# Eight 48-wide heads laid in natural order with zero padding, loads over two queues, and a new order of single operations, in a recurrence with a bilinear layer behind it

## The chip, the cores and the metric

The kernel runs on one core of one Trainium2 chip. The metric is the device time of one execution in microseconds (us). Most executions of one kernel agree within 0.3 to 1%; some fall into a slower state with a lower granted clock on the matrix engine, and each run is marked fast or slow. Only fast runs are compared. Names: PE is TensorE (matmuls; PEld is its weight load), DVE is VectorE, ACT is ScalarE, POOL is GpSimd, SP is SyncE, and a "q" after a name means that engine's instruction queue, where it also issues DMA transfers.

## The reference

For each of 4 batches and 8 heads, a 48 x 48 state decays row by row with `alpha`, takes an outer product, and is read by the query, over 768 steps. The features of the eight heads, 384 in all, then pass a bilinear layer.

```python
B, H, S, D = 4, 8, 768, 48
for t in range(S):
    state = alpha[:, :, t, :, None] * state + einsum('bhd,bhe->bhde', k[:, :, t], v[:, :, t])
    y[:, :, t] = einsum('bhd,bhde->bhe', q[:, :, t], state)
x = y.transpose(0, 2, 1, 3).reshape(B * S, H * D)        # 3072 x 384
out = ((x @ w_a) * (x @ w_b)) @ w_out                    # 384 -> 1536 -> 384
```

## The kernel before

Both kernels cut the work into six chunks: chunk c handles two batches ("halves" 0 and 1) and 256 of the 768 steps. A chunk loads `a`, `k`, `q`, `v`, takes logarithms and prefix sums of the decays, multiplies `q` and `k` by them, and turns the products so that the feature dimension lies on the partitions. It then makes scores, masks them, adds the part carried in by the state, and gives features `xT`. Chunk c is a set of single steps; the bilinear part of earlier chunks fills TensorE between them.

The products of a chunk lie in `QKp`. There are two ways to turn them into `kqT`: eight TensorE transposes per half and per four heads, with a copy out of PSUM (`stC`), or one DMA transposition per half (`stT`), which costs TensorE nothing:

```python
def stC(ch, u, h, eng):
    t = bank("f", 4, BF16, [C, 2, 2, 2, C])
    for j, src in ((1, Kp[i]), (0, Qp[i])):
        for p in range(2):
            for r in range(2):
                nc.tensor.transpose(t[:, j, r, p], src[...], ident)
    ...                                      # copy to kqT on VectorE or ScalarE
def stT(ch, u, eng):                         # eng is SyncE
    eng.dma_start_transpose(out=alloc_t(ch, u).rearrange(...), in_=QKp[ch.c % 2][:, u].rearrange(...))
```

The decay of a whole half chunk reaches the state's layout either by 64 one-column matmuls or by a way over DRAM, on SyncE's queue too: two transfers `row <- beta`, then two `bl <- row`.

```python
def decay(ch):
    row = dram.tile([2, 2 * P2, 2, D], F32, name="row")
    for g in range(2):
        nc.sync.dma_start(out=row[g:g + 1]..., in_=ch.beta[(g + 1) * HC - 1:(g + 1) * HC, :, 1]...)
    for r in range(2):
        nc.sync.dma_start(out=bls[ch.c % 2][r * DP:r * DP + D]..., in_=row[:, :, r, :]...)
```

Heads sit in slots of 64 with 16 unused columns, so the last two heads' features must be moved into the gaps of the first six: the "gap" matmuls `stG`. The order of steps is a list per chunk of the bilinear part, of which these are some steps (cuts are marked by dots; the numbers of an entry are its place and its chunk; `T` is the DMA transposition, `C` the TensorE one, `dec D` the decay by DMA, `ld` a load, the last letter the engine):

```python
1: [... (14, 2, "C 0 0 V"), ..., (15, 2, "C 1 0 V"), ...          # chunk 2 turns on TensorE
    (18, 4, "new"), ..., (19, 4, "ld q * P"), (19, 4, "ld k * P"), ..., (20, 4, "ld v * P"), ...
    (25, 3, "mq 0 V"), (25, 3, "T 0 Y"), (26, 3, "mq 1 V"), (27, 3, "dec D"), (27, 3, "T 1 Y"), (27, 4, "ld a * P")],
```

Of the kernel before, what the change touches and what calls it, by code (L numbers as in the profile page):

```python
# [14 lines left out]
START = [  # L15
    (0, "new"), (0, "ln"), (0, "ld a 0 Y"), (0, "ld a 1 Y"), (0, "ld k 0 Y"), (0, "L 0 V"), (0, "ld q 0 Y"), (0, "warm 18"), (0, "ld v 0 Y"),
    (0, "ld k 1 Y"), (0, "ld q 1 Y"), (1, "new"), (0, "ld v 1 Y"), (0, "L 1 P"), (0, "A 0"), (0, "gate_w q 1"), (0, "W 0 512"), (0, "W 512 1024"),
    (1, "ld a * P"), (0, "W 1024 1536"), (0, "Wo 4 8"), (0, "Wo 0 4"), (0, "A 1"), (1, "ld v 0 P"), (0, "Wo 8 12"), (1, "ld k 0 P"),
    (1, "ld q 0 P"), (1, "ld q 1 P"), (0, "warm 24"), (1, "ld k 1 P"), (1, "ld v 1 P"), (0, "mk 0 V"), (0, "dec P"), (0, "v 0 S"), (0, "mq 0 V"),
    (0, "C 0 0 V"), (0, "warm 6"), (0, "C 0 1 S"), (0, "D 0 0 s2"), (0, "K 0 P y2"), (0, "warm 8"), (0, "warm 14"), (0, "v 1 S"), (0, "S 0"),  # L20
    (0, "mk 1 V"), (0, "D 0 1 s2"), (0, "mq 1 V"), (0, "warm 18"), (0, "Y 0 V"), (0, "C 1 0 V"), (0, "G 0 V"), (0, "D 1 0 s2"), (0, "C 1 1 S"),
    (0, "K 1 V y2"), (0, "ff 1 0"), (0, "ff 0 0"), (0, "S 1"), (0, "D 1 1 s2"), (0, "Y 1 S"), (0, "ff 3 0"), (0, "G 1 S"), (0, "ff 2 0"),
    (0, "ff 1 1"), (0, "ff 2 1"), (0, "ff 0 1"), (0, "ff 3 1"),
]



PLAN = {
    0: [(9, 1, "L * V"), (14, 1, "A 1"), (16, 1, "A 0"), (16, 1, "dec P"), (16, 2, "new"), (16, 2, "ld a * P"), (22, 2, "ld v * P"),
        (24, 1, "v 0 S"), (25, 1, "mk 0 V"), (25, 2, "ld k * P"), (25, 2, "ld q * P"), (25, 1, "mq 0 V"), (25, 1, "C 0 0 V"), (25, 1, "C 0 1 S"),  # L30
        (25, 1, "D 0 0 s2"), (25, 1, "K 0 P y2"), (26, 1, "mk 1 V"), (26, 1, "S 0"), (26, 1, "mq 1 V"), (26, 1, "D 0 1 s2"), (27, 1, "Y 0 S"),
        (27, 1, "v 1 S"), (27, 1, "C 1 0 V"), (27, 1, "C 1 1 V"), (27, 1, "G 0 S"), (27, 1, "D 1 0 s2"), (27, 1, "K 1 V y2"), (27, 1, "S 1"),
        (27, 1, "D 1 1 s2"), (27, 1, "ff 1 0"), (27, 1, "ff 3 0"), (27, 1, "Y 1 S"), (27, 1, "G 1 S"), (27, 1, "ff 0 0"), (27, 1, "ff 2 0")],
    1: [(0, 1, "ff 1 1"), (2, 3, "new"), (5, 1, "ff 3 1"), (5, 3, "ld k * P"), (5, 3, "ld a * P"), (6, 1, "ff 2 1"), (6, 2, "L * V"),
        (7, 3, "ld q * P"), (10, 1, "ff 0 1"), (10, 2, "A 0"), (10, 2, "A 1"), (11, 2, "mk 0 V"), (12, 2, "dec P"), (12, 3, "ld v * P"),
        (12, 2, "mq 0 V"), (13, 2, "mk 1 V"), (13, 2, "mq 1 V"), (14, 2, "C 0 0 V"), (14, 2, "v * S"), (15, 2, "C 0 1 S"), (15, 2, "C 1 0 V"),
        (15, 3, "L * P"), (16, 2, "D 0 0 s2"), (16, 2, "K * P"), (17, 2, "C 1 1 S"), (18, 2, "S 0"), (18, 4, "new"), (18, 2, "D 0 1 s2"),
        (19, 4, "ld q * P"), (19, 4, "ld k * P"), (20, 2, "D 1 0 s2"), (20, 2, "Y 0 S"), (20, 3, "A 0"), (20, 4, "ld v * P"), (21, 2, "G 0 V"),
        (21, 3, "mk 0 V"), (22, 3, "A 1"), (22, 2, "S 1"), (22, 2, "D 1 1 s2"), (23, 3, "mk 1 V"), (24, 2, "Y 1 S"), (25, 2, "G 1 S"),
        (25, 3, "mq 0 V"), (25, 3, "T 0 Y"), (26, 3, "mq 1 V"), (27, 3, "dec D"), (27, 3, "T 1 Y"), (27, 4, "ld a * P")],  # L40
    2: [(6, 3, "v * P"), (6, 3, "D 0 0 s2"), (8, 4, "L * P"), (9, 3, "K * V"), (10, 3, "S 0"), (10, 3, "D 0 1 s2"), (12, 5, "new"), (12, 3, "Y 0 S"),
        (13, 3, "D 1 0 s2"), (13, 3, "G 0 S"), (14, 4, "A 1"), (15, 3, "S 1"), (15, 3, "D 1 1 s2"), (16, 4, "A 0"), (16, 3, "Y 1 S"),
        (16, 4, "mk 0 V"), (19, 4, "mq 0 V"), (19, 4, "T 0 Y"), (20, 3, "G 1 S"), (22, 4, "mk 1 V"), (23, 4, "mq 1 V"), (24, 4, "v * S"),
        (24, 4, "dec D")],
    3: [(0, 4, "K * V"), (5, 5, "ld a * P"), (6, 5, "ld q * P"), (6, 4, "S 0"), (6, 4, "D 0 0 s2"), (7, 5, "ld v * P"), (7, 4, "D 0 1 s2"),
        (7, 5, "L * V"), (8, 4, "T 1 Y"), (9, 5, "ld k * P"), (11, 4, "D 1 0 s2"), (11, 4, "Y 0 S"), (12, 4, "G 0 S"), (12, 5, "A 0"),
        (13, 4, "S 1"), (13, 4, "D 1 1 s2"), (14, 5, "mk 0 V"), (14, 5, "A 1"), (15, 5, "mq 0 V"), (16, 4, "Y 1 V"), (16, 5, "dec D"),
        (19, 5, "mk 1 V"), (19, 4, "G 1 S"), (20, 5, "mq 1 V"), (20, 5, "T 1 Y"), (20, 5, "T 0 Y"), (26, 5, "v * V")],
    4: [(0, 5, "K * V"), (1, 5, "D 0 0 s2"), (6, 5, "D 1 0 s2"), (6, 5, "S 0"), (9, 5, "D 0 1 s2"), (12, 5, "Y 0 V"), (13, 5, "G 0 V"),
        (14, 5, "S 1"), (14, 5, "D 1 1 s2"), (17, 5, "Y 1 S"), (23, 5, "G 1 S")],  # L50
    5: [],
}


@with_exitstack
def kernel(
# [125 lines left out]
    def logs(ch, us, eng):  # L182
        if us.start == 0:
            alloc(ch)
# [301 lines left out]
```

## Time and profile before

| | before |
|---|---|
| time, median (range), first three runs | 224.5 us (222.9 to 227.1) |
| profiled span, granted clock | 222.4 us, 0.987 |
| TensorE busy | 199.5 us, 90% |
| bytes moved by DMA, packets | 30.70 MB, 37,874 |

The prediction below shows the lines that bound it, with their reading. First SyncE's queue (columns: start, time on the queue, engine, line of the kernel, operation, out<-in, how many):

```profile
99.08 3.12 SPq L264 DMA_TRANSPOSE kqT<-QKp  x1
...
104.81 1.31 SPq L221 DMA_DIRECT2D row<-beta  x2
107.34 0.93 SPq L224 DMA_DIRECT2D bl<-row  x2
```

The first DMA transposition of the whole kernel is issued at 99 us, when most of the ordinary loads are through, and holds the queue for 3.1 us.

### The profile page before, as it was taken

The page shows a single profiled execution, that of the slowest core. Times are in us where ns is not written, and L with a number is a line of the kernel's source. Part 1 is how long each engine was busy: PE and PEld are TensorE (multiplying, and loading weights), DVE is VectorE, ACT ScalarE, POOL GpSimd, SP SyncE. Part 2 cuts the span into 40 slices and gives each one's busy share as a digit, 9 for nine tenths or more (in the row PEclk, how much of TensorE's full clock was granted, in tenths as well). Part 3 has the DMA queues.
Part 4 walks back from the last instruction along what each step waited for, and adds up shares of the span by engine and source line. Part 5 has one row for each costly group of instructions (what it writes and reads, how often), then busy time and mean ns, then how long its engine had stood idle before and what let it go on. Part 6 is the DMA issues. An engine that isn't in the chain of part 4 may idle for free.

```text
span 222.4 us, 6004 instructions
## 1 busy us (share of the span) xinstructions
PE 199.5 (90%) x2558; PEld 118.5 (53%) x2584; DVE 132.0 (59%) x189; ACT 105.9 (48%) x195; POOL 55.7 (25%) x79
## 2 busy tenths in 40 slices
PE   3798799999799969899779999899999989999991
PEld 3487665566575545464345565464555445544460
DVE  5569657458736879942887914889508763045400
ACT  3470467742346955644517654577233334254420
POOL 8358949737200048400280000000000000000000
PEclk9999999999889999999999999999999999999997
DMA  7999999999999103999879945400881000320022
GB/s 168 261 175 154 200 181 168 271 266 323 325 282 259 38 3 82 265 271 180 65 173 264 197 114 113 93 0 4 126 172 37 3 3 0 83 58 3 0 71 71
DMA packets 37874, 30.70 MB, mean 138 GB/s; under 512 B 27084, under 2 KB 34008, under 8 KB 37848
## 3 DMA queue, kind: packets, MB, share of 16 engines
q0 software_dynamic: 8480, 19.27, 37.4%
q1 hardware_dynamic: 29368, 11.05, 25.6%
q8 instruction: 20, 0.33, 0.6%
q14 instruction: 6, 0.05, 0.1%
HBM read 25.97 MB, written 4.74 MB: 138 GB/s over the span
## 4 chain that ended last, share of the span: by engine, by line
PE 75%; DVE 12%; ACT 4%; issue 3%; DMA 2%; POOL 1%; SPq 1%; POOLq 0%; DVEq 0%; ACTq 0%
PE f L379 20%; PE f L360 19%; PE f L370 18%; PE f L207 4%; DVE m L282 4%; PE y L308 3%; PE s L281 3%; PE y L292 2%; PE f L254 1%; PE y L315 1%; DVE xT L297 1%; DVE kqT L260 1%; PE f L203 1%; DMA bl<-row 1%; DVE tmp L342 1%
## 5 line engine op out<-in xcount | busy, mean ns | idle before, releaser
L360 PE MATMUL f<-xT,wa_t 128*128 128x512 bf16 (+1 forms) x229 | 59.6, 361 | 1.2 <-ACT kqT L258 0.3
L370 PE MATMUL f<-xT,wb_t 128*128 128x512 bf16 (+1 forms) x225 | 59.0, 361 | 1.1 <-issue 0.5
L379 PE MATMUL f<-wo_t,prod 128*128 128x384 bf16 x288 | 48.6, 326 | 0.7 <-DVE prod L372 0.7
L379 PEld LDWEIGHTS <-prod 128*128 128x128 bf16 x288 | 27.8, 98 | 19.7 <-DVE prod L372 1.1
L360 PEld LDWEIGHTS <-wa_t 128*128 128x128 bf16 x240 | 22.5, 99 | 21.2 <-issue 1.0
L370 PEld LDWEIGHTS <-wb_t 128*128 128x128 bf16 x240 | 22.4, 99 | 21.2 <-issue 1.3
L282 DVE TENSOR_TENSOR m<-s,mask 128x1024 bf16<-128x1024 f32 x24 | 29.3, 1222 | 4.3 <-PE s L281 4.0
L381 ACT ACTIVATE ot<-f 128x384 f32<-128x384 f32 x24 | 11.8, 490 | 35.0 <-PE f L379 34.9
L187 POOL TENSOR_TENSOR l<-la 128x768 f32<-128x768 f32 (+1 forms) x3 | 4.6, 1532 | 41.1 <-ACT la L185 22.3
L299 ACT ACTIVATE xT<-y 128x256 bf16<-128x256 f32 (+1 forms) x18 | 10.7, 596 | 8.6 <-PE y L308 5.6
L207 PE MATMUL f<-l,ut_f 128*128 128x384 f32 x24 | 11.1, 562 | 3.6 <-DVE l L187 3.6
L215 DVE TENSOR_TENSOR QKp<-k_t,invb 128x768 bf16<-128x768 f32 x12 | 12.4, 1036 | 1.0 <-ACT invb L211 1.0
L281 PE MATMUL s<-kqT 64*64 64x128 bf16 x384 | 11.5, 222 | 1.4 <-DVE kqT L260 0.7
L215 DVE TENSOR_TENSOR QKp<-q_t,beta 128x768 bf16<-128x768 f32 x12 | 11.6, 977 | 0.5 <-DMA q_t<-in_q_dram 0.5
L342 DVE TENSOR_TENSOR tmp<-s,S 128x384 f32<-128x384 f32 x4 | 2.2, 558 | 15.5 <-PE s L329 15.5
L281 PEld LDWEIGHTS <-kqT 64*64 64x64 bf16 x384 | 7.7, 106 | 6.0 <-issue 3.9
L210 ACT ACTIVATE invb<-f 128x384 f32<-128x384 f32 x12 | 5.9, 492 | 10.0 <-DVE le L208 10.0
L185 ACT ACTIVATE la<-a_t 128x1536 f32<-128x1536 f32 (+1 forms) x7 | 9.1, 1295 | 3.1 <-DMA a_t<-in_alpha_dram 3.1
L208 DVE TENSOR_TENSOR le<-f,la 128x384 f32<-128x384 f32 x12 | 6.7, 556 | 4.9 <-PE f L207 4.7
L258 ACT ACTIVATE kqT<-f 128x1024 bf16<-128x1024 bf16 x5 | 5.1, 1022 | 9.0 <-PE f L254 8.9
L292 PE MATMUL y<-kqT,S 64*64 64x128 bf16 x96 | 7.0, 221 | 2.4 <-DVE tmp L342 1.5
L308 PE MATMUL y<-m,vx 64*48 64x128 bf16 x384 | 7.7, 220 | 1.6 <-DVE m L282 1.6
(233 smaller groups left out, 280.7 us busy)
## 6 DMA issues: line engine op xcount, KB each, us to landing
out_dram<-ot SPq DMA_DIRECT2D x48, 96.0 KB, 2.2
a_t<-in_alpha_dram POOLq DMA_DIRECT2D x5, 768.0 KB, 12.5
v_t<-in_v_dram POOLq DMA_DIRECT2D x4, 768.0 KB, 13.6
k_t<-in_k_dram POOLq DMA_DIRECT2D x4, 768.0 KB, 14.0
q_t<-in_q_dram POOLq DMA_DIRECT2D x4, 768.0 KB, 13.5
wo_t<-in_moe_w_out_dram POOLq DMA_DIRECT2D x3, 384.0 KB, 6.7
wa_t<-in_moe_w_a_dram POOLq DMA_DIRECT2D x6, 144.0 KB, 4.2
wb_t<-in_moe_w_b_dram POOLq DMA_DIRECT2D x6, 144.0 KB, 4.4
```

The lines of the kernel that those rows point to most:

```text
L185: nc.scalar.activation(out=ch.la[:, us].rearrange("p b h r d -> p (b h r d)"), in_=ch.a[:, us].rearrange("p b h r d -> p (b h r d)"), func ...
L207: nc.tensor.matmul(p, lhsT=ut_f32, rhs=ch.l2[:, u].rearrange("p h d -> p (h d)"), start=True, stop=True)
L215: eng.tensor_mul(dst[ch.c % 2][:, u, :, :, :D], src[:, u].rearrange("p h r d -> p r h d"), by[:, u])
L281: nc.tensor.matmul(s2[g * HC:(g + 1) * HC, r, p, rk, :], lhsT=keysT(ch, u, 2 * h + p, g, r, rk), rhs=queriesT(ch, u, 2 * h + p, g, rs), st ...
L282: nc.vector.tensor_mul(m.rearrange("p r a k s -> p (r a) (k s)"), s2.rearrange("p r a k s -> p (r a) (k s)"), maskn(4))
L292: nc.tensor.matmul(y[rs, g, p, :], lhsT=lhsT, rhs=queriesT(ch, u, p, g, rs), start=(p == 0), stop=False, skip_group_check=True)
L299: nc.scalar.activation(out=o_, in_=i_, func=AF.Copy)
L308: nc.tensor.matmul(ch.y[u][r * DP:r * DP + D, g, p, :], lhsT=ch.vx[g * HC:(g + 1) * HC, u, 2 * p + r, rk, :], rhs=ch.m[u, p // 2][g * HC:( ...
L360: nc.tensor.matmul(ap, lhsT=wa_t[:, kk, f * 128:(f + 1) * 128], rhs=ff_x(ch, us)[:, kk], start=(kk == 0), stop=(kk == KT - 1))
L370: nc.tensor.matmul(bp, lhsT=wb_t[:, kk, f * 128:(f + 1) * 128], rhs=ff_x(ch, us)[:, kk], start=(kk == 0), stop=(kk == KT - 1))
L379: nc.tensor.matmul(op, lhsT=ch.prod[:, f, m * C:(m + 1) * C], rhs=wo_t[:, f, :], start=(f == 0), stop=(f == NFF - 1))
L381: nc.scalar.activation(out=ot, in_=op, func=AF.Copy)
```

## The change

The intent is less work for TensorE and a denser start. Heads lie in natural order, 48 wide, in three tiles of 128; values and states are padded with zeros, so a head that straddles a multiple of 64 is made in two pieces and the gap matmuls go. Chunk 0 is loaded half by half over SyncE's and GpSimd's queues. Most products of `q` and `k` move from VectorE to GpSimd, chunk 2 turns by DMA as well, and the order of everything is one list of single operations over all chunks.

```diff
-    def stG(ch, u, eng):
-        for t in range(KT):
-            for g in range(2):
-                nc.tensor.matmul(ch.y[u][:, g, t, :], lhsT=gap[:, t]..., rhs=ch.xT[:, KT, 2 * g + u, :], ...)
+    PIECES = [(h, j) for h in range(H) for j in range(D * h // DP, (D * h + D - 1) // DP + 1)]
+    def inner(ch, u):
+        for n in reversed(range(len(PIECES) // 2)):
+            for rk in range(2):
+                for c in range(2):
+                    h, j = COLS[c][n]
+                    at = h * VS + DP * j - D * h
+                    for g in range(2):
+                        out_mm(ch, u, g, h, j, vx[gs, u, rk, at:at + DP], ch.m[u, h // 4][gs, h % 2, h // 2 % 2, rk, :])
...
-    (0, "ld a 0 Y"), (0, "ld a 1 Y"), (0, "ld k 0 Y"), (0, "L 0 V"), (0, "ld q 0 Y"), (0, "warm 18"), ...
+0: c1; warm 70 0; cz 0 V; cz 1 V; cs 0 V; cs 1 V
+0: ld a 0 Y; ld k 0 Y; ld q 0 Y; ld a 1 P; ld v 0 Y; ld k 1 P
...                                              (from here on cut to the lines of 60 to 115 us that matter here)
+2: dec
+2: mk 1 P
+4: ld k * P
+2: T 0
+4: ld q * P
+2: T 1
+3: E 0 b0; le 1; E 1 i1; mq 0 P; mk 0 V
+3: E 1 i0; mq 1 P; T 0
+3: dec
+3: mk 1 P
+4: ln *; ld v * P
+3: T 1
+5: ld a * P
+5: ld k * P
+3: D 0 0 4
+5: ld q * P
```

In this list the number ahead of the colon is the chunk, `mq`/`mk` the query and key product of a half, `T` its DMA transposition, `D` its scores, `dec` its decay by DMA, `P`, `V`, `S`, `Y` the engine.

## The prediction

> **What bounds the kernel now.** I read the page's busy line and the chain of waits first, then the chain in order of time, then busy time by stretches, then the timeline of the start.
>
> The page names TensorE, and the chain agrees:
>
> ```profile
> PE 199.5 (90%) x2558; PEld 118.5 (53%) x2584; DVE 132.0 (59%) x189; ACT 105.9 (48%) x195; POOL 55.7 (25%) x79
> ...
> PE 75%; DVE 12%; ACT 4%; issue 3%; DMA 2%; POOL 1%; SPq 1%; POOLq 0%; DVEq 0%; ACTq 0%
> ```
>
> Matmul ends are modelled, so for costs I take the steps in the chain in order of time (start, length, what), which are start to start:
>
> ```profile
> 12.26 0.83 PE s L236 x64
> ...
> 36.57 0.65 PE f L370 x3
> ...
> 37.86 0.65 PE f L207 x2
> ...
> 47.87 0.46 PE f L254 x8
> ...
> 116.27 0.44 PE y L315 x6
> ...
> 126.38 7.80 PE f L379 x48
> ...
> 145.06 0.45 PE y L308 x32
> ...
> 165.41 0.83 PE s L329 x55
> ...
> 170.99 0.45 PE y L292 x16
> ```
>
> So three 512-column matmuls cost 0.65 us; one prefix sum (L207, two halves) 0.65; eight transposes 0.46; six gap matmuls (L315) 0.44; 48 output matmuls 7.80; 32 value matmuls (L308) 0.45, 14 ns each; 16 carried-state matmuls (L292) 0.45, 28 ns each. Sum for the whole kernel: 144 groups of three give 93.6, 288 output matmuls 46.8, twelve prefix sums 7.8, twelve groups of transposes 5.5, 24 of scores at about 0.43 (estimate, from their 16 in 0.42 to 0.45) 10.3, L292 5.4, L308 5.4, L315 5.3, the state products about 5.0, decays on TensorE 3 x 0.83 = 2.5. **Total 187.6 us of TensorE demand** in a span of 222.4; 140.4 of it, the bilinear part, no change of layout can touch.
>
> Where are the other 35 us? In the start, in stalls, and in the tail. The stretches (columns: us, then busy time and instructions of PE, PEld, DVE, ACT, POOL, granted clock, DMA share, GB/s):
>
> ```profile
> 54.00:60.00 6.00, 4.38 (x139) 3.40 (x136) 4.06 (x7) 2.42 (x4) 3.26 (x3) 0.97 1.05 333
> 60.00:66.00 6.00, 5.51 (x69) 4.12 (x66) 2.39 (x4) 2.51 (x6) 0.00 (x0) 0.74 1.05 292
> 66.00:80.00 14.00, 12.95 (x156) 7.71 (x157) 11.34 (x19) 11.85 (x22) 0.00 (x0) 1.00 0.52 131
> 80.00:98.00 18.00, 15.63 (x286) 9.63 (x281) 14.71 (x18) 8.71 (x19) 9.49 (x8) 1.00 0.63 159
> 98.00:114.00 16.00, 13.68 (x169) 6.98 (x170) 8.72 (x11) 6.40 (x10) 4.15 (x4) 1.00 0.86 140
> 217.90:222.40 4.50, 0.00 (x0) 0.00 (x0) 0.00 (x0) 0.48 (x1) 0.00 (x0) 0.74 0.30 72
> ```
>
> The tail is 4.5 us. TensorE becomes dense only when the second half of the first chunk's features is ready, at 28.6 us (the chain's last "ACT xT L299" of the start is at 27.75, 0.82 long). By then it has done about 9.4 us of chunk 0's recurrence and eight half groups of the bilinear part at 0.325, 2.6 us: 12.0. From 28.6 to 217.9 are 189.3 us for the remaining 175.6, so **stalls and slow clock are about 13.7 us**. One clear stall is at 109.8 to 112.1, where carried-state matmuls wait for a state whose decay came by DMA: the chain has SPq 0.69, row 1.67, bl 2.30, DVE Sm 1.90 in a row there.
>
> **What the skill says.** (1) "TensorE: Matmul & The Clock Gate", Part 1: the array runs at half rate until it has been busy for about 3.4 us and falls back after such an idle window. The trace agrees: the first 18 warm-up matmuls take 2.10 us (117 ns each), the array then idles from 3.5 to 7.0, and the first two prefix sums take 2.90 us instead of 2 x 0.65. (2) "DMA: Bandwidth & Descriptors", Specifications: transfers under 512 B are below line rate. Inputs come in pieces of 384 B; they moved at 261 GB/s between 6 and 12 us, while 333 appear at 54 to 60. (3) "SBUF — State Buffer", "Who interferes with whom": a VectorE instruction with two SBUF inputs and a GpSimd instruction reading SBUF exclude each other. I use it for a rival; no view of before isolates it.
>
> **The change, part by part.**
>
> TensorE demand. The eight heads of 48 features are laid at their natural place in three tiles of 128, so a head that straddles a 64 boundary is computed in two pieces with zero padding: twelve pieces in place of eight heads. Counted from the instruction order of both kernels:
> - gap matmuls 72 to 0: minus 12 x 0.44 = -5.3
> - transposes on TensorE 96 to 64 (chunk 2 now by DMA too): -4 x 0.46 = -1.8
> - value matmuls 384 to 576: +192 x 0.014 = +2.7
> - carried-state matmuls 192 to 240. Before, each used the diagonal quarters only (input half equals output half), 28 ns; now input and output halves cross, four quarters in turn as in L308, so 14 ns (estimate): 3.4 for 5.4, -2.0
> - state products 384 to 320: -64 x 0.013 = -0.8; decay on TensorE three chunks to two: -0.8
>
> Sum **-8.0**, demand 179.6. The bilinear part only changes a few full groups into halves, at no cost (0.325 twice is 0.65).
>
> VectorE. 15 of 24 input multiplications go to GpSimd (15 x about 1.0 = -15), five PSUM copies of transposes go (-3.4), the split copies of y become single (-1.3), nine output copies come (+5), state multiplications come back from GpSimd (+3.5): about 121 for 132. ACT loses nine 0.38 copies of y, nine of 0.49 of the output and most casts of v: about 95. GpSimd gains 15 multiplications of perhaps 1.8 us (it took 1.80 for the addition of 768) to about 75. None comes near 180, so none of this counts by itself; only where they sit in a chain.
>
> The start. (a) l2 of chunk 0 still starts near 6.3 us: the mask copy (1.88) goes, but VectorE now clears both buffer sets (0.48 + 0.4 + 0.07 + 0.8 + 0.4, twice, 4.3 us, scaled from before's memsets). (b) 70 warm-ups hold TensorE until about 6.6, so the prefix sum takes 0.65, not 1.45, and the exponentials begin straight after it at 7.7 rather than 9.26. (c) Operations are single, so query and key of half 0 are ready near 11.5 (before: 12.3, and then TensorE was in decays until 13.0), masks of half 0 end near 16.6 (18.96). (d) Chunk 1's first prefix sum stands ahead of Y 0 in TensorE's order; it needs chunk 1's alpha, the fifth block on the SP queue. At about 265 GB/s for both queues together (both are the same engines) 3.1 MB of chunk 0 are in at 14 us, alpha of chunk 1 near 15, its logarithm and GpSimd's pair sum near 17.5. So Y 0 near 19, features of half 0 near 21 (21.9 now), of half 1 near 24.5 (28.6 now). (e) Weights now load over 128 partitions in one transfer, not 48 and 16, but share the engines with chunk 1: at 14 us weights begin, and 0.39 MB each take about 2.2 us, so the first two quarters are in near 22.8, just in time.
>
> I choose **24.5 us for dense work**. By then TensorE has done 8.2 of chunk 0, 2.1 of chunk 1 and seven half groups, 2.3: 12.6. Left: 179.6 - 12.6 = 167.0. Stalls: before 13.7; the new order interleaves two or three chunks' bilinear work between single steps, but TensorE is in order and each step's engine must be on time; I choose 11, in which 1.5 for waits on weights and the clock's dip. 24.5 + 167.0 + 11 + 4.5 = **207.0**.
>
> **The rivals.**
> - Loading becomes the wait. Chunk 1's inputs now compete with weights between 14 and 30 us; if 265 GB/s is all there is, 6.3 MB of two chunks plus 3.1 of early weights need until about 37 us. If the order needs them earlier, dense work starts near 30 and the time is 212 to 216. For it: DMA share is full in the first 72 us now. Against: weights in narrow transfers now reach only 173 to 187 GB/s.
> - GpSimd becomes the late partner: 15 multiplications on the slower engine, behind DMA issues of about 1.1 us each and excluded by VectorE. Each late key or query delays transposes by DMA (4.5 us). Then stalls stay at 13 or more: 210 to 214.
> - Everything is on time: stalls fall to 4, as between 160 and 217.9 now, where TensorE idles only 1.4 of 57.9 us. Then 200.
> - The granted clock falls as TensorE gets denser. The clock was 0.74 in 60 to 66 us, once; one or two more such dips cost about 1.5 us each.
>
> **Range and chances.** The TensorE saving is nearly certain and alone makes 216; the start adds 3 to 5, the order 0 to 10. Range 200 to 216. Slower needs both first rivals at full size: 0.01; within 2% 0.03; faster 0.96.
>
> **What would show it.** Right: no gap matmuls; carried-state groups at about 14 ns each; prefix sum of chunk 0 at 0.65; dense bilinear matmuls from about 24 us; TensorE idle under 9 us from there to the end. Wrong: TensorE waits on wa, wb or chunk 1's alpha before 35 us; GpSimd as releaser of TensorE or of the DMA transposes; a second clock dip; value matmuls above 14 ns, since they load weights 64 wide for pieces partly zero.

## More of the kernel before

Second the stretch from 26 to 40 us (columns as in the prediction: us, then busy time of PE, PEld, DVE, ACT, POOL with counts, granted clock, DMA share, GB/s):

```profile
26.00:40.00 14.00, 13.65 (x171) 8.81 (x173) 7.17 (x13) 9.84 (x20) 10.82 (x16) 1.00 1.07 197
```

TensorE is full there: 13.65 of 14 us.

## The result, and the profile after

| | before | after |
|---|---|---|
| time, median (range) of 4 runs | 224.89 us (222.94 to 227.13) | 231.68 us (230.98 to 258.82) |
| fast runs | all four | 231.72, 231.64, 230.98 (the fourth, 258.82, is slow: clock 0.892) |
| profiled span, clock | 222.4 us, 0.987 | 229.9 us, 0.963 |

The ratio is 1.032, 95% interval 1.023 to 1.041: the kernel is slower, where 207 us and faster had been predicted. Ratios in this document are the mean time of one kernel's fast runs over that of the other's from the same rounds, so not quite the ratio of the medians that I quote. Results are correct in every run unless I say otherwise.

The page of the changed kernel: busy time, forty slices of TensorE, clock and DMA in tenths, and the chain of waits by engine.

```profile
PE 196.6 (85%) x2641; PEld 118.4 (51%) x2664; DVE 129.4 (56%) x189; ACT 94.7 (41%) x175; POOL 67.5 (29%) x68
...
PE   8868885989999956930799999899999999999992
...
PEclk9999999999999995895599999999999999999999
...
DMA  7999999999993999999417610431340230001235
...
PE 67%; DMA 15%; DVE 5%; issue 5%; SPq 3%; POOL 2%; ACT 1%; DVEq 0%; ACTq 0%; POOLq 0%
```

Busy time of TensorE did fall, though part of it ran at a lower clock. But DMA's share of the chain rose from 2% to 15%. The slices say where: each is 5.75 us, and in slices 15 to 20, some 80 to 115 us, TensorE shows 5, 6, 9, 3, 0, 7 tenths and a clock of half speed twice, while DMA is full in slices 14 to 19. By stretches:

```profile
26.00:40.00 14.00, 9.71 (x179) 7.13 (x178) 8.26 (x12) 5.47 (x16) 10.37 (x9) 1.00 1.22 235
80.00:98.00 18.00, 13.45 (x203) 7.55 (x202) 10.87 (x13) 7.46 (x15) 12.88 (x10) 0.81 1.06 265
98.00:114.00 16.00, 5.27 (x151) 3.16 (x150) 4.79 (x7) 2.04 (x4) 0.63 (x1) 0.69 0.92 169
114.00:126.00 12.00, 11.95 (x167) 6.57 (x167) 6.52 (x8) 6.57 (x11) 5.41 (x3) 0.98 0.37 68
160.00:200.00 40.00, 39.74 (x407) 21.11 (x405) 19.73 (x28) 13.63 (x24) 0.00 (x0) 1.00 0.23 49
```

Against the lines of before (13.65; 15.63; 13.68 in the first three), TensorE lost 3.9 us early and 10.6 us of busy time from 80 to 114, more in work, since a good part of what is left ran at half clock. From 114 on it is as dense as anyone could ask. So the loss is not dearer work on TensorE (196.6 us busy for 199.5, part of it at half clock); the change starved it, for the most part in one place.

What starved it is on SyncE's queue:

```profile
74.97 1.59 SPq L692 DMA_TRANSPOSE kqT<-QKp  x1
...
78.66 10.24 SPq L692 DMA_TRANSPOSE kqT<-QKp  x2
89.00 1.27 SPq L646 DMA_DIRECT2D row<-beta  x2
95.32 0.97 SPq L649 DMA_DIRECT2D bl<-row  x2
96.40 11.94 SPq L692 DMA_TRANSPOSE kqT<-QKp  x1
...
118.43 1.51 SPq L692 DMA_TRANSPOSE kqT<-QKp  x1
```

and beside it GpSimd's queue, where it issues loads:

```profile
75.58 1.19 POOL L594 DMA_DIRECT2D k_t<-in_k_dram  x1 [2.83 <-DVE vx L706]
76.76 1.15 POOL L594 DMA_DIRECT2D q_t<-in_q_dram  x1
...
86.67 1.20 POOL L594 DMA_DIRECT2D v_t<-in_v_dram  x1
87.86 1.15 POOL L594 DMA_DIRECT2D a_t<-in_alpha_dram  x1
89.00 1.15 POOL L594 DMA_DIRECT2D k_t<-in_k_dram  x1
90.92 1.16 POOL L594 DMA_DIRECT2D q_t<-in_q_dram  x1
```

The same instruction holds the queue for 1.5 to 1.6 us at 75 and at 118, when few loads move beside it, and for 11.94 us at 96, with five loads of 0.79 MB issued beside it since 86 (four are shown, the fifth comes at 97.5; 3.9 MB; at the 265 GB/s of that stretch some 15 us, an estimate). The line at 78.66 is two turns, of 7.23 and 2.84 us. SyncE issues in order, so what comes after waits too: the decay of chunk 3 is issued at 89.0, as soon as those two are through, and the turn at 96.4, as soon as the decay is. The small transfer of the decay is slow as well: its second step can start only 6.3 us after its first, when `row` has landed, where before took 2.5 (104.8 to 107.3). TensorE's own lines, from its timeline, and the chain's piece of the same wait:

```profile
88.42 0.64 PE L749 MATMUL psum<-kqT 64*64 64x128 bf16 x16 [4.04 <-DMA kqT<-QKp]
...
110.37 0.64 PE L749 MATMUL psum<-kqT 64*64 64x128 bf16 x16 [10.51 <-DMA kqT<-QKp]
```

```profile
89.68 5.62 DMA row<-beta
96.40 13.93 DMA kqT<-QKp
```

Score matmuls stood idle for 4.0 and 10.5 us, until transposed data had landed. From issue to use the last took 13.93 us, not the 4.5 that I had carried over from before. After each such wait the clock is down. For the second, in windows of the same trace:

```profile
98.00:104.00 6.00, 1.86 (x127) 1.41 (x124) 1.02 (x2) 2.04 (x4) 0.63 (x1) 1.00 1.06 246
104.00:106.00 2.00, 0.00 (x0) 0.00 (x0) 0.00 (x0) 0.00 (x0) 0.00 (x0) 0.53 1.04 223
106.00:114.00 8.00, 3.41 (x24) 1.75 (x26) 3.77 (x5) 0.00 (x0) 0.00 (x0) 0.50 0.79 98
```

the array is idle from about 100 and granted half speed from about 104 until after 113. That is what the Trainium skill says in "TensorE: Matmul & The Clock Gate", Part 1 (half rate after an idle window of about 3.4 us), and this wait agrees. The first does not quite: TensorE stopped at 84.4, and the clock was down from about 87.1, some 2.7 us later (0.77 in 86 to 88, 0.50 in 88 to 92).

One warning on reading: the page's list of DMA issues gives a median of 4.4 us to landing for the eight transposes, as in before. The median, and only those whose landing is matched, hide the slow ones; the queue and the chain show them.

### The profile page after: what moved, and what is told of

It reads as the page before. It is cut to its first block, busy times and chain, and to the rows that moved or that the text cites.

```text
span 229.9 us, 6120 instructions
## 1 busy us (share of the span) xinstructions
PE 196.6 (85%) x2641; PEld 118.4 (51%) x2664; DVE 129.4 (56%) x189; ACT 94.7 (41%) x175; POOL 67.5 (29%) x68
## 4 chain that ended last, share of the span: by engine, by line
PE 67%; DMA 15%; DVE 5%; issue 5%; SPq 3%; POOL 2%; ACT 1%; DVEq 0%; ACTq 0%; POOLq 0%
PE psum L816 37%; PE psum L839 18%; DMA a_t<-in_alpha_dram 6%; DMA kqT<-QKp 6%; PE psum L765 5%; DMA row<-beta 2%; PE psum L623 2%; DVE QKp L641 2%; PE psum L749 2%; POOL QKp L641 2%; SPq L594 1%; PE psum L720 1%; DVE vx L706 1%; DVE prod L829 1%; SPq L692 1%
## 5 line engine op out<-in xcount | busy, mean ns | idle before, releaser
L816 PE MATMUL psum<-xT,wa_t 128*128 128x512 bf16 (+1 forms) x233 | 54.8, 355 | 3.1 <-issue 1.5
L816 PE MATMUL psum<-xT,wb_t 128*128 128x512 bf16 (+1 forms) x236 | 55.0, 355 | 2.7 <-ACT as__815 L822 1.8
L839 PE MATMUL psum<-wo_t,prod 128*128 128x384 bf16 x288 | 54.5, 335 | 0.0
L754 DVE TENSOR_TENSOR m<-psum,mask 128x1024 bf16<-128x1024 f32 x24 | 29.1, 1223 | 18.0 <-PE psum L749 16.8
L641 POOL TENSOR_TENSOR QKp<-q_t,beta 128x768 bf16<-128x768 f32 x8 | 15.6, 1959 | 29.8 <-ACT beta L637 23.9
L749 PE MATMUL psum<-kqT 64*64 64x128 bf16 x384 | 10.6, 226 | 15.7 <-DMA kqT<-QKp 14.6
L641 POOL TENSOR_TENSOR QKp<-k_t,invb 128x768 bf16<-128x768 f32 x7 | 12.7, 1812 | 17.9 <-PE psum L816 17.9
L749 PEld LDWEIGHTS <-kqT 64*64 64x64 bf16 x384 | 7.3, 110 | 18.6 <-DMA kqT<-QKp 15.2
L619 PE MATMUL psum<-wz 128*128 128x128 bf16 x148 | 11.3, 243 | 1.0 <-DVE wz L542 1.0
L765 PE MATMUL psum<-m,vx 64*64 64x128 bf16 x576 | 10.9, 225 | 0.8 <-DVE m L754 0.8
L619 PEld LDWEIGHTS <-wz 128*128 128x128 bf16 x148 | 10.3, 111 | 1.6 <-DVE wz L542 1.0
## 6 DMA issues: line engine op xcount, KB each, us to landing
q_t<-in_q_dram POOLq DMA_DIRECT2D x4, 768.0 KB, 13.9
v_t<-in_v_dram POOLq DMA_DIRECT2D x4, 768.0 KB, 13.3
```

Of the source, the lines that this page charges most:

```text
L619: nc.tensor.matmul(w[:, :C], lhsT=wz, rhs=wz, start=True, stop=True)
L641: eng.tensor_mul(QKp[ch.c % 2][:, u, j, :, :, :D], src[:, u].rearrange("p h r d -> p r h d"), by[:, u])
L749: nc.tensor.matmul(s2[g * HC:(g + 1) * HC, r, p, rk, :], lhsT=ch.kqT[u][rs, 1, rk, 2 * h + p, g * HC:(g + 1) * HC], rhs=queriesT(ch, u, 2 ...
L754: nc.vector.tensor_mul(m.rearrange("p r a k s -> p (r a) (k s)"), ch.s2[u, h].rearrange("p r a k s -> p (r a) (k s)"), maskn(4))
L765: nc.tensor.matmul(y[c * DP:(c + 1) * DP, g, j // 2 * C:(j // 2 + 1) * C], lhsT=lhsT, rhs=rhs, start=(g, c) not in begun, stop=False, skip ...
L816: nc.tensor.matmul(p, lhsT=(wa_t, wb_t)[w][:, kk, f * 128:(f + 1) * 128], rhs=ch.xT[:, kk, us, :], start=(kk == 0), stop=(kk == KT - 1))
```

## The experiments

My theory, C: a transposition by DMA that meets ordinary loads is slow, it holds SyncE's queue, and TensorE waits. Rivals: G, GpSimd's slower products make the turns late; Q, the decay by DMA stands ahead of the turn on the same queue; and, for the first 40 us, L, the loads of chunk 1 hold up the features. Every edit is to the changed kernel unless I say otherwise. All ran for three rounds, one for five; each list of intervals is a 95% interval of the ratio to the kernel before. In the edits lines of the order are shown as above.

### 1. Loads later

```diff
-5: ld k * P        (some steps after 5: ld a * P)
-5: ld q * P        (some steps later)
-5: ld v * P        (later again)
+5: ld k * P; ld q * P; ld v * P     (after 4: mk 1 P, some 20 us later)
```

> Theory C (contention): in the changed kernel the DMA transposes of chunks 2 and 3 and the decay of chunk 3 share the DMA engines with bulk loads of chunks 4 and 5 (265 GB/s from 84 to 104 us), and take 10 to 14 us instead of 4.4. Here k, q and v of chunk 5 (2.4 MB, about 9 us of the engines at 265 GB/s) are issued later, behind GpSimd's last key product of chunk 4. C expects: the transpose issued near 96 lands within 6 us, TensorE's 10.5 us idle before the scores of chunk 3 shrinks below 4, the half clock after it goes, and the time falls by 8 to 12 us, to 220 to 224. Rival G (GpSimd's products are late): no part of them moves, so the time stays within 2 us of 231.7. Rival Q (the order on the SP queue: the decay's round trip stands ahead of the transpose): the order is the same, so the time stays within 3 us.

Measured: 225.27 us (224.23 to 227.31), ratio to before 1.003 [0.994, 1.013]. That transposition on the queue:

```profile
96.71 2.86 SPq L690 DMA_TRANSPOSE kqT<-QKp  x1
```

2.86 us in place of 11.94, at nearly the same moment, with the same instructions ahead of it. Some 6 us came back by moving three loads alone. C holds for this turn; the whole gain, 6.4 us, is less than the 8 to 12 expected, and waits for turned data of 7.3 us in three pieces, the longest 4.3, are left: chunk 4's loads still lie on the second turn of chunk 2 and the first of chunk 3.

### 2. Turns on TensorE

```diff
-2: T 1      -3: T 0      -3: T 1
+c: C u 0 t; C u 1 t+1; Ce u 0 S; Ce u 1 V     (c the chunk, u the half; each just ahead of that half's D, on the same banks)
```

> Three of the four transposes of chunks 2 and 3 go to TensorE (8 transposes of 0.46 us per half group, six half groups, 2.8 us) and their PSUM copies to ScalarE and VectorE in the same place, loads and everything else as in the changed kernel. C and Q both expect: no wait for a DMA transpose between 80 and 112 us; each of the three places now waits about 1.2 us for a copy; gain 10 to 13 us, to 219 to 222, with the decay of chunk 3 by DMA as the wait that remains. G expects the waits to stay, now on GpSimd's products, and a gain under 4 us.

Measured: 222.36 us (220.52 to 223.44), ratio 0.987 [0.979, 0.995], 9.3 us below the changed kernel and so just short of the 10 to 13 expected. TensorE does 14.38 us in 98 to 114, not 5.27:

```profile
98.00:114.00 16.00, 14.38 (x130) 7.59 (x133) 9.48 (x12) 7.87 (x13) 4.80 (x3) 0.89 0.68 144
```

So paying for three halves with TensorE's own time (six groups of eight, 0.46 us each, 2.8 us) is cheaper than waiting for the DMA engines.

### 3. The products back on VectorE

```diff
-3: mq 0 P   -3: mq 1 P   -3: mk 1 P
+3: mq 0 V   +3: mq 1 V   +3: mk 1 V
```

> The three products of chunk 3 that GpSimd makes (1.81 us each) go to VectorE (0.95 us each), as in the kernel before. G expects keys and queries of chunk 3 some 3 to 5 us earlier and the idle time before the scores of chunk 3 shorter by as much: 227 to 229. C expects that the transposes then meet the same loads, which are issued behind fewer GpSimd instructions and so even earlier: within 2 us of 231.7.

Measured: 231.64 us (230.85 to 233.14), ratio 1.030 [1.023, 1.038], as the changed kernel itself. TensorE still waits, once for 15.9 us. The unchanged time alone does not clear GpSimd, since here loads were issued earlier too and the first turn, at 78.8, holds the queue for 16.0 us, not 7.2. The changed kernel's own trace does. Chunk 3's last product on GpSimd is

```profile
84.92 1.81 POOL L641 TENSOR_TENSOR QKp<-k_t,invb 128x768 bf16<-128x768 f32 x1
```

so it was done at 86.7, and its turn was issued at 96.4, 9.7 us later. G is refuted for the turn that costs most: the products were ready; the queue and the transfer were not.

### 4. The turn ahead of the decay

```diff
-3: dec      (before 3: mk 1 P)
 3: T 1
+3: dec      (after it)
```

> On the SP queue the second transpose of chunk 3 is issued ahead of that chunk's decay, nothing else moves. Q expects that it is issued near 89 instead of 96.4 us, lands 7 us earlier, and the time falls by 6 to 8 us, to 224 to 226, unless the decay takes its place as the wait. C expects it to be issued earlier but to take over 8 us beside the loads, and the decay, now behind it, to become the wait for the states of chunk 3: a gain of 0 to 4 us.

Measured: 234.59 us (233.86 to 235.06), ratio 1.042 [1.035, 1.049]. The list of waits shows what took its place:

```profile
PE psum L748 <- DVE le L627: 11.2, 1, 11.2
...
PE psum L748 <- DMA kqT<-QKp: 7.2, 2, 4.7
```

Columns are who waited, for whom, us in total, times, the longest. TensorE's waits for turned data fall from 14.6 to 7.2 us, but the turn, issued at 89.6, now holds the queue for 16.0 us, the decay is issued after it at 105.7, and ScalarE waits for it:

```profile
112.02 0.87 ACT L636 ACTIVATE beta<-psum 128x384 f32<-128x384 f32 x2 [11.85 <-DMA row<-beta]
```

This exponential of chunk 4 overwrites the `beta` that the decay has yet to read; VectorE's `le` waits for it, and TensorE's next scores for that, 11.2 us. In sum it is no faster (the two intervals overlap). The order on the queue only chooses which of two slow transfers is waited for, so the decay's place ahead of the turn is not the cause, and Q is refuted.

### 5. Both remedies

Experiment 2 with experiment 1's later loads.

> The two cures together: transposes of chunks 2 and 3 on TensorE (as e2_pe_turn, 222.4 us) and k, q, v of chunk 5 loaded later (as e1_late5). If contention is the whole cause of the stretch from 84 to 114 us, what is left there for e2 is the decay of chunk 3 behind the loads (a wait of 2.4 us near 99), and the sum gains 2 to 4 us over e2: 218 to 221. If the gains are not additive because the later loads now meet the transposes of chunk 4, it stays at 222 or above.

Measured: fast runs 221.22, 220.47, 221.58, one slow 225.53; ratio 0.980 [0.975, 0.985], at the upper edge of what was expected. TensorE does 15.33 of 16 us in 98 to 114, but only 10.70 of 12 in 114 to 126, a new hole that experiments 9, 12 and 13 are about.

### 6. The start with fewer loads (wrong result)

On experiment 5: chunk 1's second half of `k`, `q`, `v` is filled with zeros by VectorE instead of loaded, so the result is wrong (relative error 0.289).

```diff
-1: ld k 1 Y   -1: ld q 1 Y   -1: ld v 1 Y
+1: fill k 1; fill q 1; fill v 1
```

> Wrong result on purpose: e5_both without the loads of k, q and v of chunk 1's second block, which are set to zero on VectorE instead; 1.18 MB less in the first 37 us, 4.5 us of the engines at 260 GB/s. Theory L (the late start is the loading of chunk 1 in the same time as weights and chunk 0): TensorE's idle time between 26 and 42 us falls from about 5 to under 2 us, and the time by 2 to 4 us against e5_both. Rival O (the late start is the order of single steps on each engine, waiting for chunk 1's first alpha): the features of chunk 0 are ready at the same time as before, near 25 and 32 us, and the time falls by less than 1.5 us.

Measured: 222.88 fast, and slow runs of 227.59, 238.5 and 242.61. The profiled run was a slow one. Even so, features of chunk 0 are ready at 25.2 and 31.9 us, as in the changed kernel (25.2 and 31.9). That does not clear the loads: the three fills on VectorE, 0.7 us each from 12.9 to 15.2, stand where it had waited for a load, and half 0's copy of `kqT` starts at 16.0 as before. TensorE is busy for 11.38 of 14 us in 26 to 40, for 9.93 in experiment 5, but at a clock of 0.88 for 1.00, so the comparison says little. On L, and on the whole time, the run is inconclusive.

### 7. One product later

On experiment 5: VectorE's second query product of chunk 1 waits for its load and stands ahead of products that the bilinear part waits for.

```diff
-1: mq 1 V     (before 0: a 3 1 0)
+1: mq 1 V     (after 0: b 6 * 7)
```

> e5_both with one VectorE instruction moved: the query product of chunk 1's second block, which waits 1.7 us for its load near 35 us and then takes 2.5 us beside GpSimd's key product, stands behind the product of feature group 7 of chunk 0. O expects the wait of TensorE for ScalarE near 40 us (1.8 to 2.1 us) to go and a gain of 1 to 2 us. L expects the wait to come back at the next instruction that needs data: within 1 us of e5_both.

Measured: fast 219.88 and 220.59, slow 223.44 and 229.85; ratio of the fast ones 0.976 [0.971, 0.982]. In the profile of a slow run with full clock there TensorE does 11.39 of 14 us in 26 to 40, for 9.93 in experiment 5, and its wait of 1.83 us for a ScalarE copy is gone. A gain of 0.9 us on the means of the fast runs (220.24 for 221.09), two of four runs slow; the intervals of the two ratios overlap, so the gain is not shown. I kept it.

### 8. Chunk 1's preparation later

On experiment 5: all of chunk 1's prefix sums and exponentials of half 0 move behind chunk 0's last scores.

> e5_both with the first prefix sum of chunk 1 and what follows from it moved behind chunk 0's scores on TensorE, ScalarE and VectorE. O expects the features of chunk 0's first half 1.5 to 2.5 us earlier than 25.2 us, of its second half 1 to 3 earlier than 31.9, and a gain of 1 to 2.5 us. L expects the features earlier but weights or chunk 1's inputs as the new wait: a gain under 1 us.

Measured: one fast run, 221.27, three slow (225.02, 226.65, 241.29). Features are ready at 25.5 and 33.0 us: not earlier. But in this profile, of a slow run, another gap had grown, from 0.97 to 1.79 us just ahead of half 0's value matmuls, and TensorE waited 1.42 us for ScalarE before half 1. So no gain is seen, and whether chunk 1's place in the order delays the features stays open.

### 9. All of it, and chunk 2's first half on TensorE too

On experiment 7:

```diff
-2: T 0
-2: SB 0 4
+2: C 0 0 4; C 0 1 5; Ce 0 0 S; Ce 0 1 V; SB 0 4
```

> All measured gains together: the loads of the last chunk's key, query and value late, the turns of chunks 2 and 3 on TensorE (now also chunk 2's first half), and chunk 1's second query product after two VectorE products that TensorE waits for. If the loss of the changed kernel is mostly that transposes by DMA meet loads, this gives 218 to 221 us, ratio to before 0.965 to 0.982, and no wait of TensorE for kqT before 120 us. If DMA transposes were only part and the decays by DMA beside loads matter as much, it stays at 221 to 223 with slow runs among them.

Measured (five rounds): 222.96 us (221.06 to 225.15), ratio 0.998 [0.992, 1.004]. The expectation's first branch is not met; its second, 221 to 223 with a slow run, is, though experiment 10 speaks against the cause that it names. The ratio needs care: of before's twelve runs on this chip only five, 222.2 to 223.5, count as fast; the other seven, 225.9 to 227.7, were marked slow, where on other chips such times are the rule. By medians it is 0.987. But the profile too has a hole: no wait of TensorE for a DMA turn is left, and yet

```profile
114.00:126.00 12.00, 8.96 (x77) 4.44 (x67) 5.17 (x10) 5.38 (x11) 0.00 (x0) 1.00 0.97 181
```

```profile
112.21 8.26 SPq L687 DMA_TRANSPOSE kqT<-QKp  x1
```

Chunk 5's loads, put off, now lie on chunk 4's second turn, which holds the queue for 8.26 us. I took the one for the cause of the other, and experiments 12 and 13 show how wrong that was.

### 10. The decays on TensorE

On experiment 9:

```diff
-2: dec   -3: dec
+2: dk 4; de      (before 2: K * 4)      +3: dk 6; de
```

> e6_best with the decays of chunks 2 and 3 on TensorE in place of DMA (128 one-column matmuls, 1.7 us more of TensorE demand). If the decay's way by DMA holds TensorE up beside loads: a waits-for-decay gap of over 2 us goes and the time falls by 1 to 3 us against e6_best. If it is hidden already: 1 to 2 us slower, the added demand.

Measured: 225.69 us (225.07 to 226.98), ratio 1.012 [1.007, 1.018], 1.4% above experiment 9 by the ratios, 2.7 us by the medians, where 1 to 2 had been expected. The 128 one-column matmuls were reckoned at 1.7 us; the decay by DMA was hidden here, and putting it on TensorE loses.

### 11. The gaps at every 128th matmul

In the first 37 us TensorE has gaps that no wait explains ("issue"). From the changed kernel's timeline of TensorE:

```profile
16.50 0.24 PE L720 MATMUL psum<-vx,QKp 64*64 64x48 bf16 x3 [2.17 <-issue]
...
23.24 0.25 PE L749 MATMUL psum<-kqT 64*64 64x128 bf16 x3 [0.97 <-issue]
...
29.37 0.63 PE L660 MATMUL psum<-one,l 64*48 64x1 f32 x41 [1.46 <-issue]
```

Counting the recorded matmuls ahead of each gives 223, 351, 478 and, for a fourth at 35.4, 605: 128, 127 and 127 apart, some records being missing from a trace. A gap near 97 to 99 us in five variants (experiments 2, 5, 7, 8 and 14) comes after 1501, which is 223 + 10 x 128 less two missing records. The page names an instruction queue among the DMA queues:

```profile
q8 instruction: 21, 0.34, 0.7%
```

21 packets of 16 KB for 2641 + 2664 TensorE instructions is one per 253. So instructions seem to be brought in by the DMA engines, 128 pairs of load and matmul at a time. Three runs tested it, each on the best kernel at hand.

(a) Ten fewer warm-ups (on experiment 9): `warm 70 0` becomes `warm 60 0`.

> e6_best with 60 instead of 70 warm-up matmuls at the start. The unexplained TensorE gaps stand before matmuls number 224, 352, 480 and 608 of the recorded ones, exactly 128 apart, in every variant. Theory: the gap belongs to the count of instructions. Then with ten fewer it stands again before number 224, now ten matmuls later in the program (inside the 16 score matmuls), near 16.5 us, 1.9 to 2.2 us long. Rival: it belongs to that instruction or to something it waits for unseen; then it stays before the same three state-product matmuls, now number 214. Time as e6_best within 1 us under both.

Measured: 225.74 us (223.29 to 227.61), ratio 1.008 [0.999, 1.017]; the gaps moved by exactly ten matmuls. The second, for one, had stood ahead of the last three score matmuls and now stands seven matmuls into the next group of 48, leaving 41:

```profile
24.33 0.80 PE L760 MATMUL psum<-m,vx 64*64 64x128 bf16 x41 [2.06 <-issue]
```

Of the first a rest of 0.25 us stands ahead of the last nine of 16 score matmuls, ten further on as well. The gap belongs to the count of instructions, not to the step. The time is no better: the score matmuls there now wait 2.43 us for VectorE's `kqT` instead.

(b) All starting loads on one queue (on experiment 9).

> e6_best with all starting loads of chunks 0 and 1 on SyncE's queue, chunk 0's first, where GpSimd's queue carried four of chunk 0. If the gaps at every 128th matmul come from two queues filling the DMA engines at once, they fall from about 2.0, 1.0 and 1.4 to under 0.5 us and the features of half 0 come 2 to 3 us earlier than 25.1. If they come from busy DMA engines as such, they stay at 1 to 2 us, and the time is within 1 us of e6_best.

Measured: 225.32 us (224.27 to 226.04), ratio 1.010 [1.004, 1.015], 1.2% above experiment 9. The first gap is not seen, one of 2.27 us at 32 us is, and half 1's prefix sum waits 1.38 us for its data. Two queues are worth keeping; whether they make the gaps stays open.

(c) Warm-ups of 512 columns, a quarter as many (on experiment 12).

> e10_wait_landed with every group of four warm-up matmuls of 128 columns made one of 512 columns, so TensorE gets about 110 fewer instruction pairs in the first 25 us for the same busy time. If the gaps at every 128th matmul come from short instructions running faster than they can be brought in while the DMA engines are full, the gaps of the first 37 us fall from a sum of 5.8 to under 2.5 us and the features of half 0 are done by 23 instead of 25.1. If they are tied to something else: sum above 4 us. Time 1 to 3 us lower under the first, equal under the second.

Measured: 218.85 us (218.62 to 221.07), ratio 0.976 [0.968, 0.984], the same as experiment 12. Of the gaps above 0.45 us put down to "issue" in the first 37 us one of 0.60 is left, again after 478 recorded matmuls, where experiment 12 has 3.7 us and experiment 9 5.8. But what waits in the first gap's place is

```profile
16.77 0.42 PE L744 MATMUL psum<-kqT 64*64 64x128 bf16 x16 [2.44 <-DVE kqT L684]
```

and half 0's features come at 24.7 us, not by 23 (half 1's at 30.1, for 32.7 in experiment 12). So the counts fit for the gaps, and the 1 to 3 us hoped for did not come: in the first gap's place the same 2.2 us are lost to a VectorE copy that was hidden underneath. That is probably a part of the answer to the late features. In the changed kernel VectorE stands in its order before that copy at

```profile
11.88 0.95 DVE L641 TENSOR_TENSOR QKp<-k_t,invb 128x768 bf16<-128x768 f32 x1
14.28 1.84 DVE L641 TENSOR_TENSOR QKp<-q_t,beta 128x768 bf16<-128x768 f32 x1 [1.44 <-DMA q_t<-in_q_dram]
16.04 0.68 DVE L689 COPY kqT<-psum 128x1024 bf16<-128x1024 bf16 x1
```

that is, half 1's query product first waits 1.44 us for its load, then takes 1.84 us instead of 0.95 beside GpSimd's key product (at 13.49, 1.81 us long in the same trace), and only then is half 0's turn copied, though its transposes had ended by 14.0. No run moves this product alone, so what it costs in whole time is argued, not shown, and so is its part in the late features.

### 12. Loads only after the turn has landed

On experiment 9: GpSimd copies one element of chunk 4's transposed half before it issues the loads, so these cannot start earlier. Since VectorE's cast of chunk 5's values would then wait longer in its order, I moved that too.

```diff
-5: ld k * P; ld q * P; ld v * P          (after 4: mk 1 P)
+4: gl 1                                  # gpsimd.tensor_copy(go, kqT[1][0:1, 0, 0, 0, 0:1])
+5: ld k * P; ld q * P; ld v * P          (after 4: T 1)
-5: v 0 V                                 (after 5: le 0)
+5: v 0 V                                 (ahead of 5: v 1 V, some 40 operations later)
```

> e6_best, but GpSimd copies one element of chunk 4's transposed second half before it issues chunk 5's key, query and value loads, so these start only when chunk 4's transposes by DMA have landed. In e6_best the second one took 8.26 us on the queue beside these loads and TensorE did 8.96 of 12 us between 114 and 126. If that is the same loss moved, the transposition takes under 4 us there, TensorE does over 11 of 12, and the time falls by 1.5 to 3 us against e6_best, to 219 to 221.5. If that stretch's waits come from elsewhere (VectorE's products): within 1 us of e6_best.

Measured: 218.55 us (218.32 to 219.37), ratio 0.973 [0.967, 0.980], faster than before by 2.7%, all four runs fast. The turn takes 1.87 us on the queue, and TensorE is full:

```profile
114.00:126.00 12.00, 12.00 (x140) 6.00 (x138) 7.12 (x13) 7.33 (x14) 3.65 (x4) 1.00 0.88 209
```

All as expected; but two things were changed, and in experiment 9 VectorE's timeline has this:

```profile
122.12 0.56 DVE L701 CAST vx<-v_t 128x768 bf16<-128x768 f32 x1 [5.61 <-DMA v_t<-in_v_dram]
```

VectorE waited 5.61 us for a value load that I had put off in experiment 1, with the bilinear products that TensorE waits for behind it.

### 13. The cast alone

On experiment 9: only `5: v 0 V` moves; the loads stay on the turn.

> e6_best with VectorE's cast of chunk 5's first value half moved next to that of the second half, and nothing else: the loads still meet chunk 4's second turn. In e6_best VectorE idled 5.61 us for that value load and TensorE 2.88 us for a product behind it, so e10_wait_landed, which moved both the loads and this cast, does not tell which of the two helped. If the cast alone was the cause: TensorE does over 11.7 of 12 us in 114 to 126, the turn still holds the queue for over 6 us, and the time is that of e10_wait_landed, 218 to 219.5 us, span near 217.6. If the turn beside the loads was: TensorE stays below 10 of 12 and the span near 219.3.

Measured: fast 218.69, 218.81 and 219.57, one slow 224.41; ratio 0.974 [0.962, 0.987], span 216.9 us.

```profile
112.44 8.26 SPq L687 DMA_TRANSPOSE kqT<-QKp  x1
```

```profile
114.00:126.00 12.00, 11.68 (x134) 6.03 (x125) 7.21 (x12) 7.29 (x15) 0.00 (x0) 1.00 0.96 184
```

The turn is as slow as in experiment 9, landing 11.2 us after its issue, at 123.6, and it costs nothing: the scores that need it run at 124.5, with 0.9 us to spare. The hole was VectorE's wait for the load. So experiment 12 did not show what its expectation says; its gate buys margin, not time. A transposition with loads moving beside it was slow wherever I looked, and dear only where something waited for it soon. This version and experiment 12 are equal, and both beat both kernels.

### 14. Experiment 12, with chunk 2's first half by DMA

`2: T 0` as in the changed kernel.

> As e10_wait_landed, but the first half of chunk 2 stays transposed by DMA. If that one turn on TensorE buys nothing, this is equal to or up to 1 us faster than e10_wait_landed; if it meets loads, there is a wait of over 1.5 us between 84 and 92 us and slow runs above 225.

Measured: fast 219.31, 220.12 and 221.3, one slow run of 238.12; ratio 0.980 [0.972, 0.989]. Its profile has only a 0.5 us wait for that turn, so the expected one of over 1.5 us is not there; the slow run is. The two intervals overlap, so whether that one turn on TensorE pays stays open.

### 15. The converse, in the kernel before

First try: chunk 4's three loads five steps later, just ahead of chunk 3's `T 0`.

```diff
-(19, 4, "ld q * P"), (19, 4, "ld k * P"), ... (20, 4, "ld v * P")
+(25, 4, "ld q * P"), (25, 4, "ld k * P"), (25, 4, "ld v * P"), (25, 3, "T 0 Y")
```

> The converse, on the kernel before: chunk 4's key, query and value loads (2.36 MB, about 9 us at 265 GB/s) moved from three steps earlier to just ahead of chunk 3's first transposition by DMA. If transposes by DMA are slow whenever ordinary loads fill the engines, those of chunk 3 land after 9 to 14 us instead of 4.4 to 6.1, TensorE waits over 4 us for kqT, and the kernel takes 229 to 235 us, ratio 1.02 to 1.05. If the slowness belongs to the changed kernel's own layout: within 1% of before and landing below 7 us.

Measured: 225.93 us (224.95 to 227.06), ratio 1.006 [0.998, 1.013]. The profile tells why it says nothing: GpSimd issued the moved loads from 85.2 us on, and in the kernel before it issues them from 85.1 on. It had nothing to hold it, and a place in a list is not a time. By 99 us, when the turn is issued, these loads are nearly in, and it takes 3.00 us. The kernel before escapes the collision by a few us. So I forced them together, with GpSimd copying one element of chunk 3's finished query product first:

```diff
+(25, 3, "gm 0"),                         # gpsimd.tensor_copy(go, QKp[1][0:1, 0, 0, 0, 0, 0:1])
 (25, 4, "ld q * P"), (25, 4, "ld k * P"), (25, 4, "ld v * P"), (25, 3, "T 0 Y")
```

> c1_before_meets did not bring the two together: GpSimd issued the moved loads early again, and chunk 3's first transposition still took 3.00 us on the queue. Here, in the kernel before, GpSimd first copies one element of chunk 3's finished query product and only then issues chunk 4's three loads (2.36 MB, about 9 us), so they start within 1 us of chunk 3's first transposition. If transposes by DMA are slow whenever ordinary loads fill the engines, whatever the kernel: the issue of that transposition takes 7 to 12 us instead of 3.1, TensorE waits over 3 us for kqT or VectorE for row or bl, and the time is 228 to 235 us. If it belongs to the changed kernel: issue below 4 us and within 1% of before.

Measured: 232.94 us (232.26 to 233.47), ratio 1.028 [1.020, 1.037]. Its SyncE queue, TensorE's timeline, the chain and one stretch:

```profile
98.51 10.58 SPq L264 DMA_TRANSPOSE kqT<-QKp  x1
```

```profile
113.75 0.64 PE L281 MATMUL s<-kqT 64*64 64x128 bf16 x16 [8.30 <-DMA kqT<-QKp]
```

```profile
98.51 15.19 DMA kqT<-QKp
```

```profile
98.00:114.00 16.00, 7.64 (x50) 3.87 (x53) 2.06 (x3) 3.37 (x6) 4.19 (x4) 0.82 1.07 262
```

In the kernel that had no such problem, four loads issued from 96.1 on (chunk 4's alpha followed the three by itself) turn 3.12 us on the queue into 10.58, make TensorE wait 8.30 us, and cost 7 us (232.94 for 225.79 by the medians): the same form as the change's own loss, with nothing else of the change in it. (The three loads also come some 11 us later than before; what that alone costs was not tried.)

## Why the prediction was wrong

The step that failed is "Each late key or query delays transposes by DMA (4.5 us)", in the second rival, together with "I choose 11" for the stalls. I took the duration of a transposition from a kernel where it met few loads and moved it to 75 to 108 us, where two chunks' loads filled the engines, without asking what the new order puts beside it. There it takes 13.9 us from issue to use (15.2 in the converse). I did list loading as a rival, but only for the start, and DMA full in the first 72 us as its evidence; I never laid the new positions of `T` against those of `ld`.

The sum, as an estimate. From ratios, 1.032 less 0.973, the remedies of experiment 12 are worth 0.059 x 225 = 13.3 us net, nearly all of it the loss around 80 to 114 us (TensorE is busy 12.6 and 15.3 us in 84 to 98 and 98 to 114, where the changed kernel has 10.0 and 5.3). They themselves cost eight groups of transposes on TensorE, 8 x 0.46 = 3.7 us, and four waits of 0.67 to 0.78 for the copies, 2.8 us. So the collisions with their half clock cost about 20 us, of which perhaps one is experiment 7's. Then 231.7 - 20 leaves 212, five above the prediction. Of these:

- **Carried-state matmuls.** Predicted "14 ns (estimate)", since quarters alternate. From start to start that is so for the groups of twelve; the first and the last of one group are

```profile
99.49 0.22 PE L765 MATMUL psum<-kqT,S 64*64 64x128 bf16 x1
...
99.64 0.22 PE L765 MATMUL psum<-kqT,Sm 64*64 64x128 bf16 x1
```

That is twelve starts within 0.15 us, 14 ns each. Only the groups of six of chunks 0 and 1, where half of the quarters are absent, take 23 to 28 ns each. For 240 some 4.1 us, an estimate, not 3.4: 0.7 us.
- **Features of half 0 near 21, of half 1 near 24.5.** Measured 25.2 and 31.9. "Query and key of half 0 are ready near 11.5" was early by about one (the products end at 12.0 and 12.8). What failed is (d), that only chunk 1's alpha was asked about: it came at 18.7, not 15, and the chain waits for it. Moving its steps out of the way (experiment 8) brought the features no earlier, but other gaps took their place there. VectorE's place of half 1's query product, beside GpSimd's, and the gaps of TensorE are seen at the start; how much each costs, and rival L, stay open.
- **"I choose 24.5 us for dense work".** TensorE is dense from about 42 us only, but with only 4.3 us idle between 26 and 40. What is left of the five, some 4.3 us, is put to the start as the remainder, not measured.

What was right: no gap matmuls; value matmuls at 14 ns (48 in 0.67 us); carried-state matmuls at 14 ns, but for the first groups; TensorE nearly idle-free from 114 us (0.26 of 40 us idle in 160 to 200); tail about 4.5. The third step of the start, the warm prefix sum, started at 8.04, not near 7, and took 0.72 us from its start to the next step, for 0.65. "GpSimd becomes the late partner" was refuted for the turn that costs most (experiment 3), and so was my belief that TensorE's demand alone, "nearly certain", would make 216: a saving in the bound engine's work shows only where nothing else comes to bound it.

The second clock dip, named as a sign of being wrong, came: in my rival it was to come from a denser TensorE; it came after an idle one. VectorE's total came to 129.4 us, not about 121.

The Trainium skill's rule in "SBUF — State Buffer", "Who interferes with whom", that I used for a rival, fits the durations: a VectorE product takes 0.95 us alone, and one of equal size 1.84 us beside GpSimd's.

## What to carry to other kernels

A duration read from a profile belongs to what ran beside it: before moving a DMA transposition or a small transfer, lay its new time against the bulk loads, take the larger figure if they meet, and ask how soon anything needs it. Where one matmul group waits for it at once, TensorE's own transposes are the cheaper way. And when a remedy puts loads off, look who waits for them, on every engine that works in order: here a cast on VectorE, and behind it the matmuls.

## What the Trainium skill lacked or had wrong

- "DMA: Bandwidth & Descriptors", Latency and other measured facts, gives a bandwidth for DMA transposes, but I found no page that gives its time beside ordinary loads. Here a half chunk's turn holds SyncE's queue for 1.4 to 3.6 us and lands after 4.4 to 6.1 us with few loads beside it, and beside loads (1 MB or more moved meanwhile) holds it for 5.7 to 16.0 us (the longest in experiments 3 and 4), lands after 11.2 and 11.4 us in experiments 13 and 9 and, in the changed kernel and the converse, is used 13.9 and 15.2 us after its issue. All behind it on that queue waits; a decay of 3 KB had its second step 6.3 us after its first instead of 2.5.
- "Runtime: NRT & Kernel Launch", Instruction fetch mechanics, says that instructions come in during the run, in blocks of 16 KB or 256 instructions, and that the fetch is mostly hidden. The count agrees, one packet of 16 KB per 253 recorded instructions. The hiding may not hold here: gaps of 1 to 2.2 us recur at every 128th matmul while short matmuls run and DMA is full; fewer, longer warm-ups took them from 3.7 to 0.6 us. That it is the fetch is argued from the counts, not shown, and why the kernel before shows none in its start stays open.
- "SBUF — State Buffer", "Who interferes with whom", agrees with the trace; it gives two ratios, but none for such a pair. Here the exclusion, as far as durations tell, made a 0.95 us product of VectorE 1.84 us long beside a 1.81 us product of GpSimd.
- "TensorE: Matmul & The Clock Gate", Part 1, agrees with one wait: idle from about 100 us, clock 0.53 in 104 to 106 and 0.50 in 106 to 114. But half clock came too about 2.7 us after TensorE stopped at 84.4, and in experiment 12 after a gap of 1.9 us (0.57 in 16 to 20), while in experiment 9 a gap of 2.0 us at the same place left it at 1.00.
